# Duo attention into a gated MLP on one core: w_out's last quarter is issued one load sooner on GpSimd's queue

## The chip, the cores and the metric

The kernel runs on one core of a Trainium2 chip. The core has a matrix engine (TensorE, PE in the profile), three engines for element-wise work (VectorE or DVE, ScalarE or ACT, GpSimd or POOL), an engine that only issues transfers (SyncE or SP), and 16 DMA engines that all queues share. The metric is the device time of one execution in microseconds. It was 230.12 us as the median of 3 runs (229.97 to 230.5).

## The reference

Attention over 4 batches, 8 heads, 768 positions and a head size of 64, and on its output a gated MLP with 512 inputs, 2048 hidden units and 512 outputs. Three heads (0, 2, 6) see all earlier positions; the other five see the first 4 positions and a window of 64.

```python
scores = scale * np.matmul(q, k.transpose(0, 1, 3, 2))
stream_keep = causal & (is_sink | in_win)          # 5 of 8 heads; the others: causal
a = np.exp(scores - max) / sum
x = np.matmul(a, v) as (B * S, H * D)              # 3072 x 512
h = x @ w_in                                       # 512 x 2048
g = h * (1.0 / (1.0 + np.exp(-beta * h)))
out = g @ w_out                                    # 2048 x 512
```

## The kernel before

The work is cut into 8 chunks (a batch and a half of the positions, 384 rows each) and each chunk into 4 units (a pair of heads). A unit has scores (`steps_QK`: matmuls at L482, the exponential on ACT at L489 and L491, masks on DVE), then sums of values (`steps_PV`: matmuls at L563, normalised on DVE at L572 and L576 into `x`). When a chunk's `x` is whole it is transposed to `xT` (by DMA at L591, or on TensorE), and the MLP of that chunk follows: `steps_G1` multiplies by `w_in` (L631) and makes the gate `gT` with ACT (L636) and DVE (L639); `steps_G2` multiplies by `w_out` (L684), sixteen matmuls for 128 rows of output, four for each quarter of `w_out`; ACT evicts (L688) and SP stores (L690).

Both weights come in quarters of 512 KB in bf16: `load_w_in(i)` (L141) and `load_w_out(i)` (L145) issue one quarter each, on GpSimd's queue, which casts from f32 on the way. The same queue carries the row loads: from chunk 3 on, keys and queries are not transposed on TensorE but loaded as rows in bf16 (`load_rows`, L284: for keys and then for queries three row blocks of two loads, 64 KB each, so twelve loads a chunk) and then transposed by DMA on SP (L300 for keys into `KT`, L303 for queries into `QTD`). Three transposes of keys and three of queries serve a chunk; each needs two row loads. Values (`vs`) are loaded by SP (L133), cast by DVE or GpSimd into `VX` (L253), and GpSimd copies parts of them for the window heads into `VO` (L261, L262).

The order of all instructions is written out by hand. The string `RAMP` holds a word for each step of the first chunks: `wo3` is w_out's fourth quarter, `ro3` the next row load of chunk 3, `mm` and `mA` a step of the MLP, `cx` a copy of `xT`, `qk`, `ex` and `pv` scores, exponential and sums of a unit. From chunk 2 on the list `PLAN` takes over. A word's instructions go to the end of their engine's queue, so the order of two words matters only for engines that both use.

GpSimd's loads share eight semaphores, DMASW0 to DMASW7, in turn. A load that reuses one waits, on GpSimd, until the load eight before it has landed; GpSimd's later work queues behind that wait. The order of GpSimd's loads is w_in's four quarters (DMASW0 to 3), then w_out's quarters and chunk 3's row loads.

Of the kernel before, what the change touches and what calls it, by code (L numbers as in the profile page):

```python
# [18 lines left out]
def kernel(  # L19
# [792 lines left out]
    def feed(x):  # L812
# [21 lines left out]
        tq7 kk7v ex4.0 tq6 ex5.0 qk5.1 xx1 ex5.1 kq6v ad6.0 wi3 qk6.0 ad6.1 cv1.0a qk6.1 ko7 kq7v hm cx1v ex6.0  # L834
        ma5.v ex6.1 ml1 cv1.1g mm lq2.1 mlg cv1.2g pv4 vo1 lv3.0 hf wo0 rk mm pv4 ad7.0 ma5.1 qk7.0 pv4 no4 lv3.1
        ad7.1 ex7.0 pv5 rq pv5 wo1 qk7.1 lv3.2 pv5 pv7 no5 pv6 pv6 wo2 pv7 pv6 ml1 ex7.1 no6 mm pv7 no7 xx2 cx2a mA
        mA xx3 ro3 mm wo3 cx3v mA mm mm mm mA mm mA mm mm mA ro3 mm ro3 mm mA mm mm ro3 cq8g mm ck8g mA mm mm mA mm
        ro3 mm mm ro3 mA mA mb mb tt8 mb mb mb
    """
    words = RAMP.split()  # L840
# [113 lines left out]
```

## Time and profile before

| | |
|---|---|
| median of 3 runs | 230.12 us (229.97 to 230.5) |
| the profiled execution | 229.89 us |
| its span, first to last instruction | 228.2 us |
| granted TensorE clock | 0.997 |
| busy: PE, DVE, ACT, POOL | 97%, 61%, 68%, 38% of the span |
| GpSimd's DMA queue (q0) | 8.13 MB, 41.4% of 16 engines' span |
| SP's DMA queue (q1) | 22.82 MB, 50.6% |

All durations in what follows are of the profiled execution. In a timeline row stand the start, the duration, the engine, the line, the operation, what it writes and reads, the number of merged instructions, and in brackets how long the engine sat idle before it and what ended that. A GpSimd row named DMA_DIRECT2D is the issuing of a load, not its transfer. In a row of waits stand the total in us, how many times, and the longest; in a row of a queue the packets, the MB and the share of the 16 DMA engines.

### The profile page before, as it was taken

What the parts mean: (1) busy time and instruction counts of PE and PEld (TensorE: products, weight loads), DVE (VectorE), ACT (ScalarE), POOL (GpSimd) and SP (SyncE); (2) the same over time, 40 slices, a digit from 0 to 9 for tenths busy, and PEclk for the clock granted to TensorE, in tenths of its full rate; (3) what the DMA queues carried; (4) which work ended last, traced back from release to release, by engine and by line L of the source; (5) the groups of instructions that cost most, each with busy time, mean ns of one, the idle gap of its engine ahead of it and who ended that gap; (6) DMA issues with size and microseconds to landing.
All of it is one profiled execution on the core that took longest, in us unless ns stands there. A gap on an engine that the chain in (4) does not pass through costs nothing.

```text
span 228.2 us, 5028 instructions
## 1 busy us (share of the span) xinstructions
PE 220.5 (97%) x1918; PEld 126.6 (55%) x1918; DVE 139.1 (61%) x341; ACT 154.4 (68%) x253; POOL 87.8 (38%) x139
## 2 busy tenths in 40 slices
PE   8889999979999999999999999999999999999993
PEld 3466666634555665555654665556645665456553
DVE  2578888852484679447942599557973769038600
ACT  4689788826867898358943797669876877138521
POOL 4478940558154359543059108960250000000000
PEclk9999999999999999999999999999999999999998
DMA  6999999999999799989969978499903030110012
GB/s 206 246 309 227 201 210 232 196 222 175 161 173 136 178 159 113 164 183 153 103 126 139 151 177 113 74 166 143 218 4 119 12 80 0 49 62 30 0 52 90
DMA packets 95384, 31.67 MB, mean 139 GB/s; under 512 B 81776, under 2 KB 92416, under 8 KB 95360
## 3 DMA queue, kind: packets, MB, share of 16 engines
q1 hardware_dynamic: 58880, 22.82, 50.6%
q0 software_dynamic: 35904, 8.13, 41.4%
q10 hardware_dynamic: 576, 0.40, 0.5%
q8 instruction: 15, 0.25, 0.5%
q14 instruction: 9, 0.07, 0.1%
HBM read 27.27 MB, written 6.29 MB: 147 GB/s over the span
## 4 chain that ended last, share of the span: by engine, by line
PE 76%; DMA 16%; SPq 3%; POOL 2%; issue 0%; ACTq 0%; ACT 0%; POOLq 0%
PE mm L684 34%; PE mm L631 19%; DMA w_out_sb<-in_moe_w_out_dram 10%; PE sp L631 9%; PE po L563 6%; PE sp L482 6%; DMA vs<-in_v_dram 4%; DMA s<-in_q_dram 2%; PE mm L669 2%; SPq L133 1%; SPq L120 1%; POOL w_out_sb L145 1%; PE mm L482 1%; POOL VX L253 1%; PE mm L353 0%
## 5 line engine op out<-in xcount | busy, mean ns | idle before, releaser
L684 PE MATMUL mm<-w_out_sb,gT 128*128 128x512 bf16 x368 | 86.1, 379 | 1.2 <-DMA w_out_sb<-in_moe_w_out_dram 1.2
L491 ACT ACTIVATE es<-sp 128x768 bf16<-128x768 f32 (+2 forms) x72 | 56.5, 834 | 18.4 <-PE sp L482 18.0
L631 PE MATMUL mm<-xT,w_in_sb 128*128 128x384 bf16 x348 | 64.5, 326 | 0.0
L631 PEld LDWEIGHTS <-w_in_sb 128*128 128x128 bf16 x512 | 47.8, 98 | 29.8 <-issue 0.2
L684 PEld LDWEIGHTS <-gT 128*128 128x128 bf16 x368 | 33.4, 98 | 37.3 <-issue 3.0
L636 ACT ACTIVATE th<-mm,beta_h 128x384 f32<-128x384 f32 x87 | 49.6, 587 | 6.3 <-DVE Mh L238 0.9
L639 DVE SCALAR_TENSOR_TENSOR gT<-th,mm 128x384 bf16<-128x384 f32 x87 | 46.7, 551 | 7.6 <-ACT th L636 3.8
L631 PE MATMUL sp<-xT,w_in_sb 128*128 128x384 bf16 x164 | 32.3, 326 | 0.0
L688 ACT ACTIVATE osb<-mm 128x512 f32<-128x512 f32 x23 | 13.9, 602 | 26.9 <-PE mm L684 26.6
L563 PEld LDWEIGHTS <-es 128*128 128x128 bf16 x472 | 23.4, 98 | 12.7 <-issue 0.9
L253 POOL CAST VX<-vs 128x512 bf16<-128x512 f32 x15 | 9.4, 629 | 52.7 <-DMA vs<-in_v_dram 45.8
L639 DVE SCALAR_TENSOR_TENSOR gT<-th,sp 128x384 bf16<-128x384 f32 x41 | 22.3, 552 | 5.7 <-ACT th L636 3.6
L636 ACT ACTIVATE th<-sp,beta_h 128x384 f32<-128x384 f32 x41 | 23.8, 586 | 2.3 <-PE sp L631 0.2
L563 PE MATMUL po<-VX,es 128*128 128x65 bf16 x360 | 25.0, 194 | 0.3 <-ACT es L491 0.3
L284 POOL DMA_DIRECT2D s<-in_k_dram x30 | 22.4, 760 | 3.8 <-DMA w_in_sb<-in_moe_w_in_dram 3.4
L284 POOL DMA_DIRECT2D s<-in_q_dram x30 | 22.5, 783 | 1.8 <-DMA w_out_sb<-in_moe_w_out_dram 1.0
L572 DVE RECIPROCAL rec<-po 128x6 f32<-128x6 f32 x28 | 5.4, 192 | 27.2 <-PE po L563 27.1
L482 PE MATMUL sp<-QTD,KT 64*128 64x128 bf16 (+2 forms) x258 | 18.9, 240 | 0.0
L509 DVE TENSOR_TENSOR es<-es,Mh 128x768 bf16<-128x768 bf16 (+1 forms) x26 | 15.4, 618 | 5.0 <-ACT es L491 4.4
L576 DVE TENSOR_TENSOR x<-po,rec 128x384 bf16<-128x384 f32 x28 | 15.6, 557 | 1.0
L482 PEld LDWEIGHTS <-KT 64*128 64x128 bf16 x278 | 11.2, 94 | 5.7 <-issue 3.7
L261 POOL COPY VO<-VX 128x512 bf16<-128x512 bf16 x16 | 10.0, 644 | 9.5 <-DVE VX L253 9.5
(74 smaller groups left out, 156.7 us busy)
## 6 DMA issues: line engine op xcount, KB each, us to landing
vs<-in_v_dram SPq DMA_DIRECT2D x24, 256.0 KB, 5.5
out_dram<-osb SPq DMA_DIRECT2D x23, 256.0 KB, 2.9
w_in_sb<-in_moe_w_in_dram POOLq DMA_DIRECT2D x4, 512.0 KB, 9.3
w_out_sb<-in_moe_w_out_dram POOLq DMA_DIRECT2D x4, 512.0 KB, 16.7
s<-in_k_dram POOLq DMA_DIRECT2D x30, 64.0 KB, 4.9
s<-in_q_dram POOLq DMA_DIRECT2D x30, 64.0 KB, 5.9
s<-in_k_dram SPq DMA_DIRECT2D x4, 384.0 KB, 10.3
s<-in_q_dram SPq DMA_DIRECT2D x4, 384.0 KB, 10.1
```

The lines of the kernel that those rows point to most:

```text
L253: copy(out=VX[b % 2][:, h2 * HT + t, :, 0:D], in_=staged["v", c][:, t])
L284: nc.gpsimd.dma_start(out=ROWS[c % 2, name][:, t, i * 4 * D:(i + 1) * 4 * D].rearrange("p (h d) -> p h d", d=D), in_=src[b, i:H:2, r:r + 1 ...
L482: nc.tensor.matmul(sps[i][r][:, x * 128:y * 128], key(a, lhs), s["QT"][half(a), qi * 128:(qi + y - x) * 128], start=first, stop=first or y ...
L491: nc.scalar.activation(out=views[i].rearrange("p r k j -> p r (k j)"), in_=banks[2][:, :, 0:n * 128], func=ACTF.Exp, scale=scale)
L509: eng.tensor_mul(ev[:, :, 0:n], ev[:, :, 0:n], Mh[h2][:, None, m0:m0 + n].to_broadcast([128, 2, n, 128]))
L563: nc.tensor.matmul(po[:, qi, hh, :], e, val, start=(j == 0), stop=(j == len(lst) - 1))
L576: nc.vector.tensor_mul(xg[g][:, :, :, u % 2, :].rearrange("p a t d -> p t a d"), po[:, :, :, 0:D], rec.to_broadcast([128, HT, 2, D]))
L631: nc.tensor.matmul(hp[:, 0:HALF], w_in_sb[:, mo, fi * 128:(fi + 1) * 128], xT[c][:, mo, :], start=(mo == 0), stop=(mo == MO - 1))
L636: nc.scalar.activation(out=th, in_=hp[:, 0:HALF], func=ACTF.Tanh, scale=beta_h[:, fi:fi + 1])
L639: nc.vector.scalar_tensor_tensor(out=gTs[c][:, fi, :], in0=th, scalar=1.0, in1=hp[:, 0:HALF], op0=ALU.add, op1=ALU.mult)
L684: nc.tensor.matmul(op, gTs[c][:, fi, ns * 128:(ns + 1) * 128], w_out_sb[:, fi, :], start=(fi == 0), stop=(fi == FO - 1))
L688: nc.scalar.activation(out=osb, in_=op, func=ACTF.Copy, scale=0.5)
```

## The change

In `RAMP` one `ro3` and the word `wo3` change places. Between them stands one `mm`, which has nothing for GpSimd.

```diff
-        mA xx3 ro3 mm wo3 cx3v mA mm mm mm mA mm mA mm mm mA ro3 mm ro3 mm mA mm mm ro3 cq8g mm ck8g mA mm mm mA mm
+        mA xx3 wo3 mm ro3 cx3v mA mm mm mm mA mm mA mm mm mA ro3 mm ro3 mm mA mm mm ro3 cq8g mm ck8g mA mm mm mA mm
```

GpSimd's queue before, from w_out's first quarter to the second query load (`s_558` is the tile of chunk 3's key rows, `s_601` that of its query rows; in brackets, the semaphores that the row waits for):

```order
L145 DMA w_out_sb<-in_moe_w_out_dram 128x4x512 x3
L284 DMA s_558<-in_k_dram 128x4x64
L145 DMA w_out_sb<-in_moe_w_out_dram 128x4x512 [waits DMASW0_49]
L284 DMA s_558<-in_k_dram 128x4x64 [waits DMASW1_49]
L284 DMA s_558<-in_k_dram 128x4x64 [waits DMASW2_49]
L284 DMA s_558<-in_k_dram 128x4x64 [waits DMASW3_49]
L248 CAST qkb<-s_360 128x2x3x64 [waits DMAHW6_49,PE_49]
L248 CAST qkb<-s_360 128x2x3x64 [waits DMAHW5_49]
L284 DMA s_558<-in_k_dram 128x4x64 [waits DMASW4_49]
L284 DMA s_558<-in_k_dram 128x4x64 [waits DMASW5_49]
L284 DMA s_601<-in_q_dram 128x4x64 [waits DMASW6_49]
L284 DMA s_601<-in_q_dram 128x4x64 [waits DMASW7_49]
```

The same stretch of GpSimd's queue with the change:

```order
L145 DMA w_out_sb<-in_moe_w_out_dram 128x4x512 x4
L284 DMA s_558<-in_k_dram 128x4x64 [waits DMASW0_49]
L284 DMA s_558<-in_k_dram 128x4x64 [waits DMASW1_49]
L284 DMA s_558<-in_k_dram 128x4x64 [waits DMASW2_49]
L284 DMA s_558<-in_k_dram 128x4x64 [waits DMASW3_49]
L248 CAST qkb<-s_360 128x2x3x64 [waits DMAHW6_49,PE_49]
L248 CAST qkb<-s_360 128x2x3x64 [waits DMAHW5_49]
L284 DMA s_558<-in_k_dram 128x4x64 [waits DMASW4_49]
L284 DMA s_558<-in_k_dram 128x4x64 [waits DMASW5_49]
L284 DMA s_601<-in_q_dram 128x4x64 [waits DMASW6_49]
L284 DMA s_601<-in_q_dram 128x4x64 [waits DMASW7_49]
```

The four quarters now stand together, and the first key load behind them. The last row still waits for DMASW7, but the load that carries it, eight before, was the first key load and is now w_out's fourth quarter; the first key load has DMASW0.

On SP, the stretch from a load of values to the second transpose of keys, as a piece of the difference:

```order
 L133 DMA vs<-in_v_dram 128x8x64 [waits DMAHW4_49]
 L690 DMA out_dram<-osb 128x512 [waits DMAHW5_49,Activation_49]
-L300 DMA_TRANSPOSE KT_132<-s_558 128x4x128 [waits DMAHW6_49,DMASW7_49,DMASW1_49]
+L300 DMA_TRANSPOSE KT_132<-s_558 128x4x128 [waits DMAHW6_49,DMASW1_49,DMASW0_49]
 L300 DMA_TRANSPOSE KT_132<-s_558 128x4x128 [waits DMAHW7_49,DMASW3_49,DMASW2_49]
```

Nothing moved there; the first transpose of keys names the first key load's new semaphore, and needs the first and the second key load as before. On TensorE the four matmuls with w_out's fourth quarter wait for DMASW7 instead of DMASW0. The order of TensorE, DVE, ACT and SP is the same instruction for instruction.

## The prediction

> **What bounds the kernel now.** I read the page first, for the engine that is full.
>
> ```profile
> span 228.2 us, 5028 instructions
> PE 220.5 (97%) x1918; PEld 126.6 (55%) x1918; DVE 139.1 (61%) x341; ACT 154.4 (68%) x253; POOL 87.8 (38%) x139
> ```
>
> TensorE is busy for 97% of the span, so only its idle stretches are to be had. The second view is the waits, kept to TensorE and to 50 us and later: it has one single row. The third is busy time by stretches. The fourth, TensorE's instructions around the wait, shows what that row is.
>
> ```profile
> PE mm L684 <- DMA w_out_sb<-in_moe_w_out_dram: 1.2, 1, 1.2
> ...
> 50.20:90.00 39.80, 39.80 (x388) 22.87 (x388) 24.09 (x68) 30.56 (x49) 22.09 (x30) 1.00 1.47 161
> 90.00:130.00 40.00, 40.00 (x330) 21.88 (x329) 22.66 (x60) 23.88 (x41) 19.18 (x28) 1.00 1.23 141
> 130.00:228.00 98.00, 94.45 (x782) 54.24 (x780) 56.00 (x128) 62.48 (x103) 18.76 (x25) 0.99 0.48 83
> ...
> 47.91 1.03 PE L684 MATMUL mm<-w_out_sb,gT 128*128 128x512 bf16 x4
> 50.16 1.02 PE L684 MATMUL mm<-w_out_sb,gT 128*128 128x512 bf16 x4 [1.21 <-DMA w_out_sb<-in_moe_w_out_dram]
> ```
>
> In a row of stretches the first number is its length, then come PE, PEld, DVE, ACT and POOL. After 50.2 us TensorE is never idle until its work ends (39.80 of 39.80, 40.00 of 40.00, and 94.45 of 98 with the tail behind the last matmul in it), while DVE and ACT are full for 61% and 77% of the first of them. So one thing holds TensorE after the ramp: at 50.16 the last four of a group's sixteen matmuls wait for the last quarter of w_out. The chain of work says where that quarter came from.
>
> ```profile
> 25.32 2.18 POOL w_out_sb L145 x3
> 27.50 0.69 POOL s L284
> 28.19 21.92 DMA w_out_sb<-in_moe_w_out_dram
> 50.16 3.61 PE mm L684 x16
> ```
>
> It was issued at 28.19, behind three other quarters and one load of key rows (L284), and took 21.92 us to land, at 50.11. What it did in those 21.92 us is read from GpSimd's own instructions, which wait for the landings of earlier loads in the same queue (a load reuses the semaphore of the eighth load before it):
>
> ```profile
> 27.46 0.78 POOL L284 DMA_DIRECT2D s<-in_k_dram  x1
> 30.42 0.75 POOL L284 DMA_DIRECT2D s<-in_k_dram  x1 [0.70 <-DMA w_in_sb<-in_moe_w_in_dram]
> 33.87 0.74 POOL L284 DMA_DIRECT2D s<-in_k_dram  x1 [2.70 <-DMA w_in_sb<-in_moe_w_in_dram]
> 45.03 0.74 POOL L284 DMA_DIRECT2D s<-in_q_dram  x1 [0.98 <-DMA w_out_sb<-in_moe_w_out_dram]
> 46.41 0.74 POOL L284 DMA_DIRECT2D s<-in_q_dram  x1 [0.64 <-DMA s<-in_k_dram]
> ...
> q0 software_dynamic: 4127, 2.83, 79.8%
> q1 hardware_dynamic: 4134, 2.08, 44.3%
> ```
>
> These releases are, in order: w_in's third quarter, w_in's fourth, w_out's third, the key load that stands ahead of w_out's fourth, and then (on TensorE, 50.16) w_out's fourth. They come in the order of issue, so GpSimd's queue (q0) hands its loads over one behind the other. The last two rows, the queues from 28 to 51 us, say that it never empties there: its packets and those of SP's queue (q1) pass one for one, 4127 to 4134. In this queue a quarter takes 33.87 - 30.42 = 3.45 us, or (45.03 - 33.87) / 3 = 3.72 us as a mean of three, and the key load 46.41 - 45.03 = 1.38 us.
>
> **The change, part by part.** It removes and adds no instruction and no byte: the key load and w_out's fourth quarter change places in one queue.
>
> *The quarter lands sooner.* Its place is taken up by 1.38 us, what the key load needs there: 50.16 - 1.38 = 48.78 for the release of TensorE. Put together the other way, from w_out's third quarter at 45.03 plus 3.45 to 3.72, it is 48.48 to 48.75. TensorE could use it at 47.91 plus four matmuls; one matmul is (3.61 - 1.02) / 12 = 0.216 us (sixteen in the chain's last row against four in TensorE's), so 48.77. Both ways it is there in time to 0.01 us, and the gain is the whole 50.16 - 48.77 = 1.39 us. The lower bound is what the earlier issue alone gives, 28.19 - 27.46 = 0.73 us, had the queue nothing to hand over; a loss in this term is excluded, since the quarter is issued sooner and has less ahead of it. I take 1.35, next to the upper end, since it is the queue's own spacing that the rows show and not the issue; the 0.04 is for a quarter that drains a little slower beside other packets.
>
> *The key load lands later*, about when the quarter did, at 50.1 instead of 46.1. The first reader of these rows is SP's first transpose of keys:
>
> ```profile
> 54.22 4.53 SPq L300 DMA_TRANSPOSE KT<-s  x3
> 59.49 6.56 SPq L303 DMA_TRANSPOSE QTD<-s  x3
> ```
>
> The transposes start at 54.22, and the first of them needs the second key load too, which lands behind both and isn't moved. The cover is 4 us: nothing.
>
> *A wait changes its object.* The eighth load ahead of the second query load was the key load, and is now the quarter. GpSimd issued that query load at 46.41; now it stands until 45.03 plus 3.45 to 3.75, 48.5 to 48.8, up to 2.4 us later. Queued behind it:
>
> ```profile
> 47.14 0.63 POOL L261 COPY VO<-VX 128x512 bf16<-128x512 bf16 x1
> 49.51 1.18 POOL L261 COPY VO<-VX 128x512 bf16<-128x512 bf16 x2 [1.74 <-DVE VX L253]
> 50.74 1.46 POOL L262 COPY VO<-VX 4x1536 bf16<-4x1536 bf16 x1
> 52.16 2.22 POOL L284 DMA_DIRECT2D s<-in_q_dram  x3
> 54.55 0.89 POOL L284 DMA_DIRECT2D s<-in_q_dram  x1 [0.18 <-issue]
> 55.85 0.74 POOL L284 DMA_DIRECT2D s<-in_k_dram  x1 [0.41 <-DMA s<-in_k_dram]
> ...
> 64.22 0.19 PE L563 MATMUL po<-VO,es 128*128 128x65 bf16 x1
> 71.22 0.61 PE L482 MATMUL sp<-QTD,KT 64*128 64x384 bf16 x8
> ...
> L303 SPq DMA_TRANSPOSE QTD<-s x1: 1190/1190/1190, 64.9 to 64.9; - x1
> DMA to landing us min/median/max: 2.9/2.9/2.9
> ```
>
> GpSimd stood idle for 1.74 us there anyway: 48.8 + 0.74 + 0.63 + 1.18 + 1.46 = 52.8 for the start of the three loads, against 52.16; 55.0 against 54.55 for the next; and by 55.85, where it waits for a landing, it has caught up. The copies (VO) are first read at 64.22, 11 us on. The query loads stand in a queue that still has five key loads to hand over, so a later issue is hidden by that backlog; without it, their readers are the three transposes from 59.49 (the third at 64.9, 2.9 us to land, 67.8) and the scores at 71.22, which keep 71.22 - 67.8 = 3.4 us, or 2.1 when TensorE comes 1.35 sooner. I cost it at nothing.
>
> *From 50 us to the end.* With TensorE unbroken from here, the 1.35 us reach the end if no input stays behind. DVE and ACT work on TensorE's products and have room; SP's transposes of x are issued when DVE has made x from TensorE's sums. The closest of these has no slack at all:
>
> ```profile
> 121.05 1.21 SPq L591 DMA_TRANSPOSE xT<-x  x1
> 126.61 0.88 PE L631 MATMUL mm<-xT,w_in_sb 128*128 128x384 bf16 x4
> ...
> L591 SPq DMA_TRANSPOSE xT<-x x1: 1212/1212/1212, 121.0 to 121.0; - x1
> DMA to landing us min/median/max: 5.9/5.9/5.9
> ...
> DMA to landing us min/median/max: 2.8/4.6/6.6
> ```
>
> Issued at 121.05, it lands at 126.95, in the middle of the four matmuls that begin at 126.61. It starts from TensorE's own sums, so it moves with them, and its 5.9 us are near the longest that a transpose of x took (6.6 in the last row, which is of all of them).
>
> The sum: 1.35 us off the profiled execution, which took 229.89 us (a span of 228.2 and 1.7 around it), is 228.54. That execution lies 0.23 below the median of the runs, 230.12, so the forecast for the median is 230.12 - 1.35 = 228.8.
>
> [...]
>
> **The rivals.**
>
> *The queue counts bytes, not loads.* Then the key load is worth its share of a quarter's time:
>
> ```profile
> w_out_sb<-in_moe_w_out_dram POOLq DMA_DIRECT2D x4, 512.0 KB, 16.7
> s<-in_k_dram POOLq DMA_DIRECT2D x30, 64.0 KB, 4.9
> ```
>
> 3.72 x 64 / 512 = 0.47 us, and 229.65, at the edge of what can be told. For it: the key load has an eighth of the bytes. Against: its own release stands 1.38 us behind that of the quarter ahead of it, and both loads consist of as many pieces (128 partitions of four runs). [...] Only the earlier issue's 0.73 us would give 229.4.
>
> *The gain is given back at 127.* If GpSimd's and SP's later loads kept their hours while x comes 1.35 us sooner, the transpose of 121.05 would meet more of them. At the longest of its kind, 6.6, it gives back 0.7 (229.5); it must take 7.25 us to give back all (230.1). For it: no slack. Against: in SP's order its loads and transposes stand between output stores, which follow TensorE, so they move along.
>
> *Slower: the queries come late.* The delayed query loads could be overtaken by the burst of key transposes, so that the third query transpose lands as late as the longest of the fifteen:
>
> ```profile
> L303 SPq DMA_TRANSPOSE QTD<-s x15: 1188/1190/1664, 59.5 to 156.8; - x15
> DMA to landing us min/median/max: 2.4/3.2/7.3
> ```
>
> 64.9 + 7.3 = 72.2, against TensorE there at 71.22 - 1.35 = 69.87: a wait of 2.3, and 228.8 + 2.3 = 231.1. It decides from a landing at 71.22 on; against it speak the backlog and the 3.4 us.
>
> **How the numbers follow.** The forecast has 77 in 100: its gain is read from the very wait that it removes, by two ways that agree. The issue's 0.73 alone has 4, the queue of bytes 5, the gain lost at 127 (with most of it gone) 6, the late queries 8. A measurement here can tell about 0.2%, 0.46 us. Faster: 77 + 4 = 0.81; same: 5 + 6 = 0.11; slower: 0.08. The likeliest case alone runs from 228.4 to 229.1 (1.39 and the 0.3 us by which runs differ; 1.0 were the quarter 0.4 slower). The range reaches on to 229.6, over the case of 229.4, and to 228.3 below; it leaves out the other rivals' 19.
>
> **What would show it.** In the trace after: no wait of TensorE for w_out; the matmuls of 50.16 at about 48.8; GpSimd's second query load near 48.8, waiting for w_out and no longer for a key load; the scores of 71.22 near 69.9 and the end 1.35 sooner. The forecast is wrong if that wait still has over 0.5 us, or if TensorE has a new idle stretch between 59 and 72 or at 125.

## The result, and the profile after

The changed kernel took 228.47 us (228.16 to 229.68, 6 runs) against 230.0 for the kernel before on the same chip (229.95 to 230.5, 6 runs): a ratio of 0.9938, with an interval from 0.9914 to 0.9962. Faster by 1.53 us was measured; 1.35 was forecast. The profiled execution took 228.31 us, and its page begins:

```profile
span 226.6 us, 5028 instructions
PE 220.1 (97%) x1918; PEld 126.5 (56%) x1918; DVE 138.7 (61%) x341; ACT 154.4 (68%) x253; POOL 87.7 (39%) x139
```

No engine's work has changed by more than 0.4 us, and the span is 1.6 us shorter. Most of what went is idle time of TensorE, 1.2 us; its busy time is 0.4 less. The view of waits, kept to TensorE from 40 us on, now has no row at all. TensorE's own rows at the place of the old wait, at the first scores that need query rows, and at the transposed `x` that had no slack:

```profile
47.75 4.48 PE L684 MATMUL mm<-w_out_sb,gT 128*128 128x512 bf16 x20
...
69.68 0.61 PE L482 MATMUL sp<-QTD,KT 64*128 64x384 bf16 x8
...
125.07 0.81 PE L631 MATMUL mm<-xT,w_in_sb 128*128 128x384 bf16 x4
```

The twenty matmuls stand in one unbroken row; before, four of them stood at 47.91 and the rest from 50.16 on. The scores moved from 71.22 to 69.68 and the MLP's matmuls from 126.61 to 125.07, both by 1.54. GpSimd's rows show what the change did in the queue:

```profile
25.25 2.97 POOL L145 DMA_DIRECT2D w_out_sb<-in_moe_w_out_dram  x4
28.19 1.52 POOL L284 DMA_DIRECT2D s<-in_k_dram  x2
30.32 0.75 POOL L284 DMA_DIRECT2D s<-in_k_dram  x1 [0.62 <-DMA w_in_sb<-in_moe_w_in_dram]
33.81 0.74 POOL L284 DMA_DIRECT2D s<-in_k_dram  x1 [2.74 <-DMA w_in_sb<-in_moe_w_in_dram]
...
45.25 0.74 POOL L284 DMA_DIRECT2D s<-in_q_dram  x1 [1.30 <-DMA w_out_sb<-in_moe_w_out_dram]
48.70 0.74 POOL L284 DMA_DIRECT2D s<-in_q_dram  x1 [2.71 <-DMA w_out_sb<-in_moe_w_out_dram]
49.44 1.83 POOL L261 COPY VO<-VX 128x512 bf16<-128x512 bf16 x3
51.34 1.46 POOL L262 COPY VO<-VX 4x1536 bf16<-4x1536 bf16 x1
52.75 3.11 POOL L284 DMA_DIRECT2D s<-in_q_dram  x4
56.08 0.75 POOL L284 DMA_DIRECT2D s<-in_k_dram  x1 [0.22 <-issue]
```

The third quarter releases GpSimd at 45.25 and the fourth, now directly behind it, at 48.70: 3.45 us. The second query load waits for that quarter, as forecast, and by 56.08 GpSimd stands where it stood before (55.85). The landings of the fourth quarter and of the key load that it passed, as answers for their tiles:

```profile
L145 POOL DMA_DIRECT2D w_out_sb<-in_moe_w_out_dram x1: 770/770/770, 27.5 to 27.5; - x1
DMA to landing us min/median/max: 21.0/21.0/21.0
...
L284 POOL DMA_DIRECT2D s<-in_k_dram x1: 777/777/777, 28.2 to 28.2; - x1
DMA to landing us min/median/max: 22.1/22.1/22.1
```

The quarter landed at 27.5 + 21.0 = 48.5, the key load at 28.2 + 22.1 = 50.3.

### The profile page after: what moved, and what is told of

It reads as the page before. It is cut to its first block, busy times and chain, and to the rows that moved or that the text cites. A ratio compares the mean times of both kernels' runs of the same rounds, so it can differ in the third digit from the quotient of the medians.

```text
span 226.6 us, 5028 instructions
## 1 busy us (share of the span) xinstructions
PE 220.1 (97%) x1918; PEld 126.5 (56%) x1918; DVE 138.7 (61%) x341; ACT 154.4 (68%) x253; POOL 87.7 (39%) x139
## 3 DMA queue, kind: packets, MB, share of 16 engines
q1 hardware_dynamic: 58880, 22.82, 50.1%
q0 software_dynamic: 35904, 8.13, 41.3%
## 4 chain that ended last, share of the span: by engine, by line
PE 87%; DMA 6%; SPq 3%; POOL 1%; issue 0%; ACTq 0%; ACT 0%; POOLq 0%
PE mm L684 36%; PE mm L631 24%; PE sp L631 12%; PE po L563 6%; PE sp L482 6%; DMA vs<-in_v_dram 5%; DMA s<-in_q_dram 2%; PE mm L669 2%; SPq L133 1%; SPq L120 1%; PE mm L482 1%; PE mm L353 1%; PE mm L601 1%; POOL VX L253 1%; POOL VO L262 0%
## 5 line engine op out<-in xcount | busy, mean ns | idle before, releaser
L684 PE MATMUL mm<-w_out_sb,gT 128*128 128x512 bf16 x368 | 85.9, 379 | 0.0
L684 PEld LDWEIGHTS <-gT 128*128 128x128 bf16 x368 | 33.4, 98 | 36.0 <-issue 1.5
```

The costliest lines, as they stand in the source:

```text
L684: nc.tensor.matmul(op, gTs[c][:, fi, ns * 128:(ns + 1) * 128], w_out_sb[:, fi, :], start=(fi == 0), stop=(fi == FO - 1))
```

## The experiments

Eight kernels were run, in two groups, each group on one chip beside the kernel before. The first four ask what the gain consists of and whether any of it is lost later; the other four ask why a load of 64 KB was worth more than a microsecond, and how much cover the delayed query loads had. In the kernels with a new helper the line numbers stand 5 or 6 higher (L689 or L690 for L684).

**The changed kernel once more**

> The changed kernel once more, to be compared with the three kernels beside it. One lane per queue: 228.5 (0.993 of before), the quarter landing about 1.4 to 1.7 us sooner than before and no wait of TensorE on it. Queue of bytes: 229.5. Issue alone: 229.3.

228.40 us (228.34 to 228.47, 6 runs) against 229.93 for the kernel before: 0.9932 (0.992 to 0.9943). The same gain on a second occasion, with a narrower interval: 1.3 to 1.8 us.

**The kernel before, with the wait taken away by other data**

```diff
-                    nc.tensor.matmul(op, gTs[c][:, fi, ns * 128:(ns + 1) * 128], w_out_sb[:, fi, :],
+                    nc.tensor.matmul(op, gTs[c][:, fi, ns * 128:(ns + 1) * 128], w_out_sb[:, fi % 12, :],
```

> The order before, but every matmul that should read w_out's fourth quarter reads its first quarter again, so that nothing waits for the fourth (which is still loaded); the output is not the reference's. This measures the whole worth of the wait. If the change gains by the wait and nothing else: 228.5, the same as the changed kernel within 0.2. If the changed order gains or loses something elsewhere as well (the queries' loads, GpSimd's copies), the two differ: were this one over 0.3 faster, the change gives something back; were it slower, the change has a second gain.

The order of all queues is the old one; the matmuls that need w_out's fourth quarter multiply by the first quarter instead, in the same number and of the same size. The same edit stands at L669.

```profile
47.91 4.48 PE L684 MATMUL mm<-w_out_sb,gT 128*128 128x512 bf16 x20
```

228.48 us (228.16 to 228.62), 0.9934 (0.9922 to 0.9945): the time of the changed kernel, with none of its new order. So the gain is that one wait, to within the 0.3 us or so that such a comparison can tell, and the new order shows no loss elsewhere. (The output of this kernel is not the reference's.)

**Two key loads ahead of the quarter**

```diff
-        mA xx3 ro3 mm wo3 cx3v mA mm mm mm mA mm mA mm mm mA ro3 mm ro3 mm mA mm mm ro3 cq8g mm ck8g mA mm mm mA mm
+        mA xx3 ro3 mm ro3 wo3 cx3v mA mm mm mm mA mm mA mm mm mA mm ro3 mm mA mm mm ro3 cq8g mm ck8g mA mm mm mA mm
```

> The kernel before, with a second key load put ahead of w_out's fourth quarter. One lane per queue: the quarter lands 1.4 to 1.7 us later than before, TensorE waits 2.6 to 2.9 us for it, 231.4 to 231.7. Queue of bytes: 0.47 more, 230.5. Issue alone: 0.73 more, 230.7.

```profile
51.68 2.10 PE L684 MATMUL mm<-w_out_sb,gT 128*128 128x512 bf16 x9 [2.66 <-DMA w_out_sb<-in_moe_w_out_dram]
```

The wait is 2.66 against 1.21 with one load ahead: the second load adds 1.45 us, much the same as the first. The time is 231.76 us (231.41, 231.5, 232.01 and 234.19), 1.0101 (1.0062 to 1.014). The last of the four lies well above the rest. It has no trace, but its mean granted clock was 0.989 where the other three have 0.996 to 1.0, and that is the clock of the run with 1024 pieces below, where the trace shows what it costs.

**The new order, but the quarter issued late**

```diff
+    def rest(n):
+        for _ in range(n):
+            nc.gpsimd.memset(idle_g, 0.0)
...
-        mA xx3 wo3 mm ro3 cx3v mA ...
+        mA xx3 ps5 wo3 mm ro3 cx3v mA ...
```

> The changed order, but GpSimd does five spare memsets (an estimated 2 to 3 us, from 0.3 us for 128x256 bf16) between w_out's third and fourth quarter, so that the quarter keeps its place in the queue and is issued later than in the kernel before. One lane per queue: the place decides and not the issue, the quarter lands as in the changed kernel, 228.5. Issue alone: it lands 2 to 3 us later than in the changed kernel, 230.0 or more.

Five fills of a 128x512 tile stand on GpSimd ahead of the quarter. GpSimd's rows:

```profile
27.69 2.90 POOL L293 MEMSET idleg<- 128x512 f32 x5
30.54 0.74 POOL L145 DMA_DIRECT2D w_out_sb<-in_moe_w_out_dram  x1
...
48.70 0.80 POOL L284 DMA_DIRECT2D s<-in_q_dram  x1 [2.77 <-DMA w_out_sb<-in_moe_w_out_dram]
```

Issued at 30.54, over 3 us later than in the changed kernel (27.5), the quarter releases GpSimd at the same 48.70. 228.50 us, 0.9934 (0.9922 to 0.9945). Its place in the queue decided, and the 3.04 us by which it was issued later cost nothing: the queue was still handing over the third quarter, which released GpSimd at 45.19.

**A spare load of 64 KB ahead of the quarter, in pieces of three sizes**

Three kernels add one load of 64 KB (as it lands, in bf16) to the changed kernel, directly ahead of w_out's fourth quarter. The length of its runs differs: 128 pieces (one run of 256 numbers for each partition), 512 (four runs of 64, as a key load has) or 1024 (eight runs of 32). The first reads from `w_out` in DRAM, the other two from the keys; what the source alone does was not tried. The page of the run with 1024 shows the pieces: GpSimd's queue has 36944 packets there, against 35904 in the changed kernel, 1040 more, which is the pieces and 16. For the other two the count is that of the runs in their edits.

```diff
+        nc.gpsimd.dma_start(out=spare, in_=moe_w_out[0:128, 0:256])          # 128 pieces
+        nc.gpsimd.dma_start(out=spare..., in_=k[3, 0:H:2, 0:128, :]...)      # 512 pieces
+        nc.gpsimd.dma_start(out=spare..., in_=k[3, 0:H, 0:128, 0:32]...)     # 1024 pieces
...
-        mA xx3 wo3 mm ro3 cx3v mA ...
+        mA xx3 sl wo3 mm ro3 cx3v mA ...
```

> As spare_512, the same 64 KB in 128 pieces (one run of 256 a partition). If the queue's time goes by pieces: between 1.38 / 4 = 0.35 us and a quarter of what a quarter of w_out needs, 3.44 / 4 = 0.86 us; TensorE waits 0 to 0.6 us, 228.5 to 229.1. If it goes by bytes: as spare_512, 229.9.

> The changed kernel with a spare load issued ahead of w_out's fourth quarter: 64 KB of keys in 512 pieces (128 partitions, four runs of 64), as a key load has them, into a tile that nothing reads. All theories: as long as the key load stood there in the kernel before, the quarter lands about 1.4 us later than in the changed kernel, TensorE waits about 1.2 us, 229.9.

> As spare_512, the same 64 KB in 1024 pieces (eight runs of 32 a partition). If the queue's time goes by pieces: twice the key load's 1.38 us, the quarter lands about 2.8 us later than in the changed kernel, TensorE waits 2.4 to 2.8 us, 231.2 to 231.5. If it goes by bytes: as spare_512, 229.9.

GpSimd's rows again give the spacing: the first is released by w_out's third quarter, the second by the spare load, the third by the fourth quarter. With 512 pieces:

```profile
45.07 0.74 POOL L284 DMA_DIRECT2D s<-in_k_dram  x1 [1.86 <-DMA w_out_sb<-in_moe_w_out_dram]
46.45 0.74 POOL L284 DMA_DIRECT2D s<-in_q_dram  x1 [0.64 <-DMA spare<-in_k_dram]
50.44 0.74 POOL L284 DMA_DIRECT2D s<-in_q_dram  x1 [3.25 <-DMA w_out_sb<-in_moe_w_out_dram]
```

With 1024 pieces:

```profile
45.09 0.74 POOL L284 DMA_DIRECT2D s<-in_k_dram  x1 [1.98 <-DMA w_out_sb<-in_moe_w_out_dram]
47.98 0.74 POOL L284 DMA_DIRECT2D s<-in_q_dram  x1 [2.15 <-DMA spare<-in_k_dram]
51.83 0.74 POOL L284 DMA_DIRECT2D s<-in_q_dram  x1 [3.10 <-DMA w_out_sb<-in_moe_w_out_dram]
```

With 128 pieces:

```profile
44.91 0.74 POOL L284 DMA_DIRECT2D s<-in_k_dram  x1 [1.99 <-DMA w_out_sb<-in_moe_w_out_dram]
45.69 0.74 POOL L284 DMA_DIRECT2D s<-in_q_dram  x1
49.15 0.74 POOL L284 DMA_DIRECT2D s<-in_q_dram  x1 [2.71 <-DMA w_out_sb<-in_moe_w_out_dram]
```

The spare load's landing stands 46.45 - 45.07 = 1.38 us behind the third quarter's in 512 pieces, to the digit what the key load had before, and 47.98 - 45.09 = 2.89 in 1024. In 128 pieces it had landed before GpSimd came to ask (the row at 45.69 has no wait), so the spacing is at most 45.69 - 44.91 = 0.78. What counts for TensorE is the landing of the fourth quarter. In the order of 128, 512 and 1024 pieces it released GpSimd at 49.15, 50.44 and 51.83 us, against 48.70 in the changed kernel. That is 0.45, 1.74 and 3.13 us later, 3.1 to 3.5 ns for each added piece (one execution each). The bytes on the core's side are the same 64 KB in all three, so for runs of 32 to 256 numbers the delay went by the pieces and not by the bytes. It was not a fixed price for a load either, which would have been the same three times.

A spacing of landings is not the time in which a load's pieces move. Before the change, between the release by the third quarter and that by the key load, the queues passed this (44.8 to 46.1 us):

```profile
DMA packets 374, 0.30 MB, mean 229 GB/s; under 512 B 52, under 2 KB 374, under 8 KB 374
q0 software_dynamic: 187, 0.17, 78.6%
```

A piece of the key load is 128 B as it lands, and only 52 packets of both queues were under 512 B. So most of the key load's 512 pieces had passed earlier, and w_out's were moving by then. What holds the key load's own landing back until then is not shown.

The waits that these loads gave TensorE, and the times:

```profile
48.90 3.40 PE L689 MATMUL mm<-w_out_sb,gT 128*128 128x512 bf16 x15 [0.25 <-DMA w_out_sb<-in_moe_w_out_dram]
...
50.20 2.10 PE L689 MATMUL mm<-w_out_sb,gT 128*128 128x512 bf16 x9 [1.37 <-DMA w_out_sb<-in_moe_w_out_dram]
...
51.58 4.65 PE L689 MATMUL mm<-w_out_sb,gT 128*128 128x512 bf16 x13 [2.72 <-DMA w_out_sb<-in_moe_w_out_dram]
```

| pieces ahead of the quarter | TensorE idle | time, us | ratio to before |
|---|---|---|---|
| 128 | 0.25 | 228.64 (228.49 to 228.74) | 0.9935 (0.9916 to 0.9955) |
| 512 | 1.37 | 229.93 (229.55 to 230.04) | 0.9991 (0.998 to 1.0002) |
| 1024 | 2.72 | 232.92 (232.67 to 233.06) | 1.0118 (1.0095 to 1.0142) |

A load like a key load in the key load's old place gives back the whole gain. With 1024 pieces the wait is as large as was expected, but the time lies above the 231.2 to 231.5 expected, and some 1.8 us above what the wait explains: 228.4 + 2.7 = 231.1. Busy time by stretches of that kernel shows the rest (the seventh figure, behind the five engines' busy times, is the granted clock):

```profile
50.00:55.00 5.00, 3.42 (x10) 1.29 (x10) 0.00 (x0) 1.00 (x2) 3.11 (x5) 0.73 1.63 160
55.00:58.00 3.00, 3.00 (x23) 1.47 (x22) 0.91 (x2) 0.74 (x2) 3.00 (x5) 0.88 2.31 228
58.00:90.00 32.00, 31.60 (x332) 18.61 (x335) 20.82 (x61) 25.78 (x41) 16.11 (x23) 1.00 1.46 143
```

A clock of 0.73 over 5 us and 0.88 over 3 costs, as an estimate that takes the work to go with the clock, 0.27 x 5 + 0.12 x 3 = 1.71 us, nearly all of the difference. The matmuls say the same: thirteen took 4.65 us there (51.58), and by the fifteen of the run with 128 pieces (3.40, less two of 0.216) they would be 2.97, 1.68 less. The page's row of the clock, in 40 slices of 5.8 us, has one low slice ahead of the last, a 7 from 52.1 to 57.9 us:

```profile
PEclk9999999997999999999999999999999999999998
```

**GpSimd held up ahead of the delayed query loads**

```diff
-        ro3 ro3 ck9v b cq9a dk3 b cv2.1v ...
+        ro3 ro3 ps5 ck9v b cq9a dk3 b cv2.1v ...
```

> The changed kernel with five spare memsets on GpSimd (2.9 us in late_issue) right behind the second query load, ahead of the copies of VO: it adds to the delay that the change itself gave this place on GpSimd (its copies there ended 0.6 us later). If the delay is covered, as the prediction has it: the third query transpose still lands before the scores need it, 228.4. If the queries come late (the slower rival): TensorE has an idle stretch near 70 us, over 229.

The same five fills, now behind the second query load:

```profile
49.19 3.31 POOL L293 MEMSET idleg<- 128x512 f32 x5
54.23 1.46 POOL L262 COPY VO<-VX 4x1536 bf16<-4x1536 bf16 x1
55.65 2.97 POOL L284 DMA_DIRECT2D s<-in_q_dram  x4
...
49.10 3.62 PE L690 MATMUL mm<-w_out_sb,gT 128*128 128x512 bf16 x16
...
71.03 0.61 PE L488 MATMUL sp<-QTD,KT 64*128 64x384 bf16 x8
```

The query loads were issued at 55.65, 2.9 us later than in the changed kernel (52.75). The time is 228.68 us (228.31 to 229.66, 6 runs), 0.9942 (0.9922 to 0.9963): no loss that can be told. The profiled execution happens to be the slowest of the six, 229.66, but it lost its time ahead of this place: its group begins at 49.10 instead of 47.75, and from there to the scores it takes 71.03 - 49.10 = 21.93 us, as in the changed kernel, 69.68 - 47.75 = 21.93. Nor did the delay reach the readers of these loads: the third query transpose was issued at 64.0, and the longest of the three took 5.6 us to land, so it had landed by 69.6, ahead of the scores at 71.03; in the changed kernel it landed at 63.4 + 3.1 = 66.5, ahead of 69.68. So the cover of the four query loads is at least these 2.9 us more than the change used, also for a TensorE that comes to the scores at 69.68. The second query load, ahead of the fills, was not held up further.

## Why the prediction was right

*The quarter lands sooner: right, with the size inside what can be told.* The term was 1.35 us, next to an upper end of 1.39 that TensorE could use. The wait is gone, and with its own order left alone and only the wait taken away the kernel before gains as much as the changed one: 228.48 against 228.40 and 228.47. The measured gain is 1.53, with an interval of 1.3 to 1.8 in the closer of the two comparisons, so neither 1.35 nor 1.39 is refuted. The 0.04 that was held back for a quarter that drains slower wasn't called for: it drained in 3.45 us. The two profiled executions differ by 1.58, but 0.16 of this is the ramp ahead of the wait, whose order was not changed: TensorE's group begins at 47.75 in one and at 47.91 in the other. Of the 1.54 by which the later rows moved, 1.38 are left for the wait.

*The two ways to the landing.* "Its place is taken up by 1.38 us" was the weaker of them: the quarter landed at 48.5 and not at 50.11 - 1.38 = 48.73. The spacing of 3.45 behind the third quarter was exact (45.25 to 48.70), though that quarter itself released GpSimd 0.22 later than before. The margin was thin, and that it was enough is in part luck: TensorE came to use the quarter at 48.6, so a landing at 48.73 would have cost it about 0.1 us. The 1.38 us were also read as what the key load needs in the queue; they are a spacing of landings, and by the packets above most of the key load had passed before. The sum needed only the landings, so it holds.

*The key load lands later: right.* 50.3, as against 50.1 forecast, and no transpose of keys was late by it. Its answer in the trace of before gives the other half of an exchange:

```profile
L284 POOL DMA_DIRECT2D s<-in_k_dram x1: 780/780/780, 27.5 to 27.5; - x1
DMA to landing us min/median/max: 18.7/18.7/18.7
```

It landed at 46.2 then, and the quarter at 50.1, after a third quarter that released GpSimd at 45.03: 5.1 us for the pair. Now the pair takes 50.3 - 45.25 = 5.05. So the change put the pair in another order and sped up neither.

*A wait changes its object: right.* The second query load was forecast for 48.5 to 48.8 (48.70), the next three for 52.8 (52.75), the catching up for 55.85 (56.08). No cost shows, and the run with GpSimd held up shows the cover for the loads behind it: they went out 3.5 us later than before the change (55.65 against 52.16), where the change alone delays them by 0.6.

*From 50 us to the end: right.* Scores and MLP both moved by 1.54, and TensorE has no wait from 40 us on. The transpose that had no slack moved along with TensorE, as argued:

```profile
119.51 1.21 SPq L591 DMA_TRANSPOSE xT<-x  x1
...
DMA to landing us min/median/max: 5.5/5.5/5.5
```

It was issued 1.54 sooner (119.51 against 121.05) and took 5.5 us against 5.9.

*The rivals.* That the queue counts bytes is refuted by the three spare loads, for runs as short as these; that only the earlier issue counts, by the late issue with the same landing. The gain was not given back at 127, and the queries were not late. The forecast of 228.8 lies 0.33 above the median, of which 0.12 is the kernel before itself (230.12 then, 230.0 beside the changed kernel).

## What to carry to other kernels

How long the wait for the last load of this queue was hung on what stood ahead of that load: 2.66 us with two key loads ahead, 1.21 with one, none with none. The amount was read from the spacing of the landings in the queue (1.38 us for a key load), not from the hour of issue (3.04 us later cost nothing) and not from the bytes (by an eighth of a quarter's bytes it would have been 0.47 us). Ask for each load that stands ahead who needs it and when: here one with 4 us of cover stood ahead of one with none. The price of a small load in this queue went by its pieces: the same 64 KB ahead of the urgent load delayed it by 0.45 us in 128 pieces and by 3.13 in 1024.

## What was not expected of the hardware

The first thing is the price by pieces. By the spacing, small runs cost 1.38 / 512 = 2.7 ns a piece in the whole queue and 2.89 / 1024 = 2.8, whether they carry 64 numbers or 32. It is no price for pieces of any size: w_out's quarter, whose pieces are of 512 numbers, took 3.45 / 512 = 6.7 ns a piece. All of this is beside SP's queue, whose packets pass one for one with this queue's (4127 to 4134 from 28 to 51 us before the change, 579 to 569 from 44.8 to 47.7 us in the run with 1024 pieces); without such a neighbour the price was not measured. Why the same pair splits as 1.4 and 3.7 in one order and as 3.45 and 1.6 to 1.8 in the other is not shown.

The second is the clock. In the run with 1024 pieces TensorE was idle for 2.72 us, and the granted clock in the profile was lower after that, 0.73 from 50 to 55 us and 0.88 from 55 to 58; with 2.66 us of idle in the run with two key loads ahead it stayed at 1.00 over the same stretches in the profiled execution. The mean clock of a whole execution was 0.989 to 0.993 in all four with 1024 pieces and 0.989 in the one of 234.19 us with two key loads ahead; in every other execution of these kernels it was 0.996 or more. That the idle time is the cause is the author's estimate from this and was not tried by itself, and how long an idle time it takes is not shown. In this run the wait of 2.72 us came with some 1.7 us more, so the price of a wait was not its length alone.
